# A third batch's keys loaded and pooled in the prologue of a fused pooled-attention and two-layer kernel

## The chip, the cores and the metric

The kernel runs on one core of one Trainium2 chip. The metric is the device time of one execution in microseconds (us), shown as the median of several executions. The engines are TensorE (PE, matmuls), VectorE (DVE), ScalarE (ACT), GpSimd (POOL) and SyncE (SP). In this kernel SyncE issues every DMA, in the order in which the program lists them.

## The reference

Batch 8, 8 heads, 576 tokens, head size 64. Keys and values are averaged over groups of 8 tokens, which leaves 72 of each per head.

```
k_p = k.reshape(B, H, 72, 8, D).mean(axis=3);  v_p likewise
scores = q @ k_p.T / sqrt(D);  attn = softmax(scores)
x = (attn @ v_p), laid out as 4608 tokens x 512
h = relu(x @ w_in1);  x = (h * h) @ w_out1
h = x @ w_in2;  g = h if h >= 1, 0 if h <= -1, else (h + 1)**2 / 4
out = g @ w_out2
```

Both inner layers are 512 -> 2048 -> 512.

## The kernel before

**Chunks.** The 4608 tokens are cut into nine chunks of 512. For a chunk the kernel computes attention by tiles of up to 128 tokens, then the first layer's 16 hidden blocks (f = 0 to 15): a hidden product `h_mm` of 12 matmuls (`hp`, lines 633 to 635), an activation (`act1`), and two blocks later a `y_step` of 12 matmuls (`y`, lines 671 to 675). Finished y banks are copied by `y_out` (`yo`, two buffers) and stored to `x2T`. The second layer follows over all chunks. Numbers are split into a high and a low part, so that each product takes three matmuls.

**Batches and chunks.** A batch has 576 tokens, so chunk 0 is batch 0; chunk 1 is the last 64 tokens of batch 0 and the first 448 of batch 1; chunk 2 has the last 128 tokens of batch 1 as its first tile and then 384 tokens of batch 2. Each batch needs its keys pooled and transposed and its values pooled and split once.

**Pooling.** `load_k(b, p)` loads the keys of two heads (p = 0 to 3), `load_v(b, g)` a group of values (g = 0 to 2), in a tile `kv` that has one buffer. `k_pool` and `v_pool` add halves three times (`pool8`, lines 365, 367 and 369; GpSimd from the second batch on), into `kp` (four buffers) and `vp`. `k_T` transposes `kp` on PE and ScalarE writes the scaled keys to `kBD`. `v_split` makes `VH` and `VL`, and for g = 2 `LH` and `LL` (two GpSimd multiplications, lines 424 and 426). A load of a new `kv` tile waits until the pooling of the one before has read it.

**Attention of a tile.** `load_q` (two `q` buffers), `t0` (query transposes, `qps`), `t1` (scores, `sps`, then maximum and subtraction), `t3` and `t4` (softmax), `t56` (transposes `aps` and `lps`, and the split into `AH`, `AL`, `LT`), then `pv_pair` (`pvps`).

**The prologue.** Chunk 0's attention, the weights' loading and decoding (`Weights`, 16 blocks, lines 256 to 290), chunk 0's hidden blocks and chunk 1's attention are interleaved by a planner, the class `Order`. Each piece of work is a generator (a chain) that yields the engine it needs and a planned time, or an event that it waits for; the planner takes the earliest, and the order in which it emits is the order of each engine's program. A load's landing is planned by `comes(us)`: the sum of transfers so far, plus `us`, plus 2.0. `keys1` is the chain that loads and pools the second batch's keys and values (b = 1); `keys1_T` transposes those keys. Chunk 1's first groups of x are staged in DRAM (`x1S`, line 623) and brought back by `unstage` (line 598) when the last weights are decoded, since x of chunk 1 lives in buffers that the decoding uses. The last weights (f = 15) land in a buffer that is lent, before that, to chunk 1's first and last tile (`late`).

**Behind the prologue.** `attention_units(c, at)` makes a list of calls with due times, in units of hidden blocks, for chunk c; the main loop over c and f executes those that are due (`do`). For each chunk that meets a new batch it lists the batch's loads, poolings and transposes: the first key load 7 units before the batch's predecessor has its scores. Chunk 2's units run beside chunk 1's blocks, which begin at unit 16. All units due at 16 or before come at the first `do(16)`, behind chunk 1's first hidden product and ahead of the last `y_step` of chunk 0.

Of the kernel before, what the change touches and what calls it, by code (L numbers as in the profile page):

```python
# [48 lines left out]
class Order:  # L49
# [13 lines left out]
    def add(self, gen, rank=0.0):  # L63
        c = [rank, self.now, gen, None, None]
        self.chains.append(c)
        self.go(c)
# [57 lines left out]
def pooled_attention_moe_moe2(  # L124
# [13 lines left out]
    nc = tc.nc  # L138
# [5 lines left out]
    NP = H // 2  # L144
# [44 lines left out]
    for c in range(NC):  # L189
        gs, col = [], 0  # L190
        while col < N:
            t0_ = c * N + col
            b, s = t0_ // S, t0_ % S
# [135 lines left out]
    def kv_tile():  # L329
        return att.tile([P, 2, POOL * D], F32, tag="kv", name="kv")  # L330

    def load_k(b, p, t=None):

        t = kv_tile() if t is None else t
        nc.sync.dma_start(
            out=t[:SP_], in_=k[b, 2 * p:2 * p + 2].rearrange("h (s r) d -> s h (r d)", r=POOL)
        )
        kraw[b, p] = t

    def load_v(b, g, t=None):  # L340

        t = kv_tile() if t is None else t
        for e in range(2):
            r = slice(64 * e, 64 * e + 64)
            if g < 2:
                src = v[b, 4 * g + e:4 * g + e + 3:2, :KA * POOL, :]
                nc.sync.dma_start(out=t[r], in_=src.rearrange("h (s r) d -> s h (r d)", r=POOL))
            else:
                src = v[b, :, KA * POOL:, :]
                nc.sync.dma_start(out=t[r, 0], in_=src.rearrange("h (s r) d -> h s (r d)", r=POOL))  # L350
        vraw[b, g] = t
# [9 lines left out]
    def pool8(eng, t, dst):  # L361
        us = (("POOL", 1.3), ("POOL", 0.8), ("POOL", 0.7)) if eng is nc.gpsimd else (
            ("DVE", 0.7), ("DVE", 0.45), ("DVE", 0.3))
        yield us[0]
        eng.tensor_tensor(out=t[:, :, :256], in0=t[:, :, :256], in1=t[:, :, 256:], op=ALU.add)
        yield us[1]
        eng.tensor_tensor(out=t[:, :, :128], in0=t[:, :, :128], in1=t[:, :, 128:256], op=ALU.add)
        yield us[2]
        eng.tensor_tensor(out=dst, in0=t[:, :, :64], in1=t[:, :, 64:128], op=ALU.add)
# [3 lines left out]
    def k_pool(b, p, eng):  # L373
        kp = att.tile([P, 2, D], F32, tag="kp", name="kp", bufs=4)
        t, dst = kraw.pop((b, p))[:SP_], kp[:SP_]
        yield from pool8(eng, t, dst)
        kp_t[b, p] = kp
# [14 lines left out]
    def v_pool(b, g, eng):  # L392
        t = vraw.pop((b, g))
        w = 2 if g < 2 else 1
        vp = att.tile([P, 2, D], F32, tag="vp", name="vp") if b else lent[7][:, 0, 2 * D * g:2 * D * g + 2 * D]
        if b == 0:
            vp = vp.rearrange("p (a d) -> p a d", d=D)
        vp_t[b, g] = vp
        yield from pool8(eng, t[:, :w], vp[:, :w])

    def v_split(b, g, eng):
        vp = vp_t.pop((b, g))
        if g < 2:
            for e in range(2):
                r = slice(64 * e, 64 * e + 64)
                vh, vl = VH[r, 2 * g:2 * g + 2, e, :], VL[r, 2 * g:2 * g + 2, e, :]
                yield "ACT", 0.33
                nc.scalar.activation(out=vh, in_=vp[r], func=AF.Copy, scale=VSCALE)
                yield "DVE", 0.32
                nc.vector.scalar_tensor_tensor(  # L410
                    out=vl, in0=vp[r], scalar=VSCALE, in1=vh, op0=ALU.mult, op1=ALU.subtract
                )
        else:
            vh = att.tile([P, 1, D], F32R, tag="vlh", name="vlh")
            yield "ACT", 0.27
            nc.scalar.activation(out=vh, in_=vp[:, 0:1], func=AF.Copy, scale=VSCALE)
            vl2 = vp[:, 1:2]
            yield "DVE", 0.23
            nc.vector.scalar_tensor_tensor(
                out=vl2, in0=vp[:, 0:1], scalar=VSCALE, in1=vh, op0=ALU.mult, op1=ALU.subtract  # L420
            )
            mb = mask.rearrange("p (h o) -> p h o", o=1).to_broadcast([P, H, D])
            yield "POOL", 1.1
            eng.tensor_tensor(out=LH, in0=vh.to_broadcast([P, H, D]), in1=mb, op=ALU.mult)
            yield "POOL", 1.1
            eng.tensor_tensor(out=LL, in0=vl2.to_broadcast([P, H, D]), in1=mb, op=ALU.mult)
        order.signal("v", b, g)
# [21 lines left out]
    def at_once(chain):  # L449

        if chain is None:
            return
        value = None
        while True:
            try:
                kind, x = chain.send(value)
            except StopIteration:
                return
            value = None
            if kind == "take":  # L460
                value = order.things[x].pop(0)[1]
# [260 lines left out]
    def attention_units(c, at, stage=(0, 0.5, 1, 1, 2, 2.5, 3)):  # L722

        units = []
        ts = tiles[c]

        def add(s, f, *a):
            units.append((s, lambda: at_once(f(*a))))

        for i, T in enumerate(ts):  # L730
            s = at[i]
            if i:
                add(at[i - 1] + 0.5, load_q, T)
            else:
                add(s - 2, load_q, T)
            add(s + stage[0], t0, T)
            add(s + stage[1], t1, T, 0)
            add(s + stage[1], t1, T, 1)
            add(s + stage[2], t3, T)
            add(s + stage[3], t4, T)  # L740
            add(s + stage[4], t56, T)
            G = T.group
            if T is G.tiles[-1]:
                for p in range(NP):
                    add(s + stage[5 + p // 2], pv_pair, G, p)
            if i + 1 < len(ts) and ts[i + 1].b != T.b:

                b = T.b + 1
                a = s + stage[1]
                add(a - 7, load_k, b, 0)  # L750
                for p in range(NP):
                    add(a - 6 + 1.5 * p, k_pool, b, p, nc.gpsimd)
                    if p + 1 < NP:
                        add(a - 6 + 1.5 * p, load_k, b, p + 1)
                    else:
                        add(a - 6 + 1.5 * p, load_v, b, 0)
                    add(a + 0.5 + p // 2 * 0.5, k_T, b, p)
                e = s + stage[6]
                add(a, v_pool, b, 0, nc.gpsimd)
                add(a, load_v, b, 1)  # L760
                add(e, v_split, b, 0, nc.gpsimd)
                add(e, v_pool, b, 1, nc.gpsimd)
                add(e, load_v, b, 2)
                add(e + 1, v_split, b, 1, nc.gpsimd)
                add(e + 1, v_pool, b, 2, nc.gpsimd)
                add(e + 1.5, v_split, b, 2, nc.gpsimd)
        return units
# [5 lines left out]
    with tc.manual_schedule():  # L773
# [19 lines left out]
        def comes(us):  # L793

            landed[0] = max(landed[0], order.now) + us
            return landed[0] + 2.0
# [23 lines left out]
        def ev(*name):  # L820
            return "ev", name
# [45 lines left out]
        def keys1():  # L867
            for p in range(NP):
                load_k(1, p)
                yield "until", comes(1.3)  # L870
                yield from k_pool(1, p, nc.gpsimd)
                order.signal("kp", p)
            for g in range(3):
                load_v(1, g)
                yield "until", comes(2.2)
                yield from v_pool(1, g, nc.gpsimd)
                yield ev("x", G1[0])
                yield from v_split(1, g, nc.gpsimd)

        def keys1_T():  # L880
            yield ev("scores", T1[0])
            for p in range(NP):
                yield ev("kp", p)
                yield from k_T(1, p)
# [121 lines left out]
        for t in T1:  # L1006
            order.add(tokens(t), RANK[1])
        order.add(keys1(), RANK[1])
        order.add(keys1_T(), RANK[1])
        for g in G1:  # L1010
# [6 lines left out]
        for c in range(2, NC):  # L1017
            n = len(tiles[c])
            stride = 3 if n > 4 else 3.5
            units += attention_units(c, [16 * (c - 1) - 1 + stride * i for i in range(n)])  # L1020
# [91 lines left out]
```

## Time and profile before

| | |
|---|---|
| median of 3 executions | 1809.26 us (1808.73 to 1817.22) |
| profiled execution, device time | 1810.97 us |
| its span, first to last instruction | 1809.2 us |
| PE busy | 1746.8 us (97%) |
| PEld / DVE / ACT / POOL busy | 80% / 41% / 43% / 8% |
| PE, busy tenths in 40 slices of 45 us | 5897699999999999999999999999999999999999 |
| granted PE clock, same slices | 6999799999999999999999999999999999999999 |

A digit of a slice is the busy share in tenths (9 is 90% or more). The clock is in tenths of the full one. In the rows below an idle time in square brackets is that of the engine just in front of the instruction, with what ended it; "x" counts merged instructions.

### The profile page before, as it was taken

To read this page: it belongs to the slowest core of one execution; us is meant where nothing else is said; L and a number is where in the kernel's file an instruction comes from. 1 tells how busy PE (TensorE), PEld (TensorE's weight loads), DVE (VectorE), ACT (ScalarE), POOL (GpSimd) and SP (SyncE) were. 2 spreads that over 40 slices of the span, in tenths; PEclk is the share of its full clock that TensorE was granted. 3 is DMA by queue.
4 is the path that set the end of the run, shared out by engine and by line. 5 is a ranking of instruction groups with operands and counts; after the bars stand their busy time and mean duration, and the time that the engine had idled before them with its cause. 6 is when DMAs were issued, how large, how long until landed. Compare 5 with 4: busy or idle time off the path is not lost.

```text
span 1809.2 us, 20648 instructions
## 1 busy us (share of the span) xinstructions
PE 1746.8 (97%) x8116; PEld 1444.9 (80%) x8116; DVE 739.0 (41%) x1234; ACT 781.5 (43%) x1499; POOL 152.1 (8%) x183
## 2 busy tenths in 40 slices
PE   5897699999999999999999999999999999999999
PEld 4676588888888888878888778888888888888887
DVE  7995243334333343433329933222223323222232
ACT  5784333434434343443348743333333333333333
POOL 3321220211111120210000000000000000000000
PEclk6999799999999999999999999999999999999999
DMA  9532310202111110311026401010101010101000
GB/s 253 175 108 67 89 34 20 67 19 59 31 52 39 38 48 18 82 21 35 1 89 214 163 0 47 1 47 1 47 1 47 1 47 1 47 1 47 0 24 24
DMA packets 89601, 95.18 MB, mean 53 GB/s; under 512 B 43296, under 2 KB 61984, under 8 KB 89504
## 3 DMA queue, kind: packets, MB, share of 16 engines
q1 hardware_dynamic: 89504, 93.87, 17.8%
q8 instruction: 64, 1.05, 0.2%
q14 instruction: 33, 0.27, 0.0%
HBM read 73.66 MB, written 20.19 MB: 52 GB/s over the span
## 4 chain that ended last, share of the span: by engine, by line
PE 86%; DVE 6%; DMA 3%; ACT 2%; issue 2%; SPq 0%; POOL 0%; DVEq 0%; ACTq 0%; POOLq 0%
PE hp L633 13%; PE hp L635 13%; PE hp L634 13%; PE y L684 7%; PE y L683 7%; PE y L682 7%; PE y L671 7%; PE y L672 6%; PE y L675 6%; PE pvps L611 2%; PE sps L502 2%; DVE w L290 1%; DVE wa L275 1%; PE qps L484 1%; PE aps L560 1%
## 5 line engine op out<-in xcount | busy, mean ns | idle before, releaser
L633 PE MATMUL hp<-x,w 128*128 128x512 f32 x1116 | 442.2, 396 | 4.6 <-ACT w L285 2.5
L634 PE MATMUL hp<-x,w 128*128 128x512 f32 x1116 | 435.7, 390 | 0.9 <-DVE w L290 0.8
L635 PE MATMUL hp<-x,w 128*128 128x512 f32 x1116 | 435.7, 390 | 0.0
L633 PEld LDWEIGHTS hp<-x,w 128*128 128x128 f32 x1116 | 210.5, 189 | 49.1 <-DVE u L661 3.0
L661 DVE SCALAR_TENSOR_TENSOR u<-u,hp 128x512 f32<-128x512 f32 x144 | 99.0, 687 | 359.7 <-ACT u L660 359.7
L635 PEld LDWEIGHTS hp<-x,w 128*128 128x128 f32 x1116 | 209.9, 188 | 44.3
L634 PEld LDWEIGHTS hp<-x,w 128*128 128x128 f32 x1116 | 210.7, 189 | 42.9 <-DVE w L290 1.5
L671 PE MATMUL y<-gh,w 128*128 128x512 f32 x576 | 232.3, 403 | 0.0
L672 PE MATMUL y<-gh,w 128*128 128x512 f32 x576 | 226.0, 392 | 0.0
L652 DVE TENSOR_TENSOR gl<-hp,gh 128x512 fp32r<-128x512 f32 x144 | 99.3, 690 | 309.8 <-ACT hp L650 309.7
L684 PE MATMUL y<-w,gl 128*128 128x512 f32 x540 | 210.2, 389 | 0.0
L682 PE MATMUL y<-w,gh 128*128 128x512 f32 x540 | 210.2, 389 | 0.0
L683 PE MATMUL y<-w,gh 128*128 128x512 f32 x540 | 210.1, 389 | 0.0
L659 ACT ACTIVATE u<-hp 128x512 f32<-128x512 f32 x144 | 85.9, 596 | 286.8 <-PE hp L635 286.8
L662 ACT ACTIVATE gh<-u 128x512 fp32r<-128x512 f32 x144 | 91.0, 632 | 173.5 <-PE y L683 148.9
L663 DVE TENSOR_TENSOR gl<-u,gh 128x512 fp32r<-128x512 f32 x144 | 99.8, 693 | 157.7 <-ACT gh L662 152.1
L675 PE MATMUL y<-gl,w 128*128 128x512 f32 x576 | 155.2, 391 | 0.0
L648 ACT ACTIVATE gh<-hp 128x512 fp32r<-128x512 f32 x144 | 86.1, 598 | 120.8 <-PE y L672 119.8
L675 PEld LDWEIGHTS y<-gl,w 128*128 128x128 f32 x576 | 108.7, 189 | 23.3
L641 ACT ACTIVATE hp<-hp 128x512 f32<-128x512 f32 x144 | 85.2, 591 | 97.5 <-PE hp L635 97.2
L671 PEld LDWEIGHTS y<-gh,w 128*128 128x128 f32 x576 | 108.9, 189 | 21.1
L672 PEld LDWEIGHTS y<-gh,w 128*128 128x128 f32 x576 | 108.9, 189 | 20.5
(140 smaller groups left out, 2003.2 us busy)
## 6 DMA issues: line engine op xcount, KB each, us to landing
w<-in_moe_w_in_dram SPq DMA_DIRECT2D x31, 512.0 KB
w<-in_moe_w_out_dram SPq DMA_DIRECT2D x31, 512.0 KB
x2T<-yo SPq DMA_DIRECT2D x36, 256.0 KB
xraw<-x2T SPq DMA_DIRECT2D x9, 1024.0 KB
out_dram<-yo SPq DMA_DIRECT2D x35, 256.0 KB
qraw<-in_q_dram SPq DMA_DIRECT2D x32, 256.0 KB
kv<-in_k_dram SPq DMA_DIRECT2D x28, 288.0 KB
kv<-in_v_dram SPq DMA_DIRECT2D x28, 256.0 KB
```

What stands on the lines that cost most here:

```text
L633: nc.tensor.matmul(out=hp, lhsT=hi[:, cs], rhs=xh[kk], start=(kk == 0), stop=False)
L634: nc.tensor.matmul(out=hp, lhsT=lo[:, cs], rhs=xh[kk], start=False, stop=False)
L635: nc.tensor.matmul(out=hp, lhsT=hi[:, cs], rhs=xl[kk], start=False, stop=(kk == KD - 1))
L652: nc.vector.tensor_tensor(out=gl, in0=hp, in1=gh, op=ALU.subtract)
L661: nc.vector.scalar_tensor_tensor(out=u, in0=u, scalar=1.0, in1=hp, op0=ALU.min, op1=ALU.max)
L663: nc.vector.tensor_tensor(out=gl, in0=u, in1=gh, op=ALU.subtract)
L671: nc.tensor.matmul(out=ys[d], lhsT=hi[:, cs], rhs=gh, start=(f == 0), stop=False)
L672: nc.tensor.matmul(out=ys[d], lhsT=lo[:, cs], rhs=gh, start=False, stop=False)
L675: nc.tensor.matmul(out=ys[d], lhsT=hi[:, cs], rhs=gl, start=False, stop=(f == KF - 1))
L682: nc.tensor.matmul(out=ys[t], lhsT=gh[:, cs], rhs=hi, start=(f == 0), stop=False)
L683: nc.tensor.matmul(out=ys[t], lhsT=gh[:, cs], rhs=lo, start=False, stop=False)
L684: nc.tensor.matmul(out=ys[t], lhsT=gl[:, cs], rhs=hi, start=False, stop=(f == KF - 1))
```

## The change

For the third batch (b = 2) the key loads, the key poolings and the first value load move from chunk 2's units into the prologue, to the end of the chain `keys1`. The other batches' stay where they are (`if b > 2`), and so do the third batch's key transposes, value poolings and splits.

```
                 a = s + stage[1]
-                add(a - 7, load_k, b, 0)
+                if b > 2:
+                    add(a - 7, load_k, b, 0)
                 for p in range(NP):
-                    add(a - 6 + 1.5 * p, k_pool, b, p, nc.gpsimd)
-                    if p + 1 < NP:
-                        add(a - 6 + 1.5 * p, load_k, b, p + 1)
-                    else:
-                        add(a - 6 + 1.5 * p, load_v, b, 0)
+                    if b > 2:
+                        add(a - 6 + 1.5 * p, k_pool, b, p, nc.gpsimd)
+                        if p + 1 < NP:
+                            add(a - 6 + 1.5 * p, load_k, b, p + 1)
+                        else:
+                            add(a - 6 + 1.5 * p, load_v, b, 0)
                     add(a + 0.5 + p // 2 * 0.5, k_T, b, p)
...
                 yield from v_split(1, g, nc.gpsimd)
+            for p in range(NP):
+                load_k(2, p)
+                yield "until", comes(1.3)
+                yield from k_pool(2, p, nc.gpsimd)
+            load_v(2, 0)
 
         def keys1_T():
```

## Rows read from the trace of the kernel before

**Rows 1.** PE's timeline, 175 to 220 us: start, duration, line, operation, count, [idle before].

```profile
189.94 1.11 PE L484 MATMUL qps<-ident,qraw 128*128 128x128 f32 x4 [14.68 <-DMA qraw<-in_q_dram]
...
195.26 0.77 PE L671 MATMUL y<-gh,w 128*128 128x512 f32 x1
...
200.53 0.44 PE L383 MATMUL kps<-ident,kp 72*128 72x72 f32 x2
...
208.20 0.47 PE L611 MATMUL pvps<-AH,VH 128*128 128x128 f32 x1 [3.77 <-DVE AL L572]
...
215.20 0.22 PE L611 MATMUL pvps<-AH,VH 128*128 128x128 f32 x1
...
216.26 0.45 PE L671 MATMUL y<-gh,w 128*128 128x512 f32 x1
...
219.07 0.60 PE L484 MATMUL qps<-ident,qraw 128*128 128x128 f32 x4
```

**Rows 2.** SyncE's timeline: DMA issues, of several merged the first's start and their length.

```profile
26.18 0.40 SPq L335 DMA_DIRECT2D kv<-in_k_dram  x1
...
66.82 1.26 SPq L347 DMA_DIRECT2D kv<-in_v_dram  x2
...
123.77 7.18 SPq L623 DMA_DIRECT2D x1S<-xs  x4
147.20 0.38 SPq L232 DMA_DIRECT2D w<-in_moe_w_in_dram  x1
...
150.51 16.06 SPq L598 DMA_DIRECT2D x<-x1S  x16
166.67 19.21 SPq L335 DMA_DIRECT2D kv<-in_k_dram  x4
185.94 0.40 SPq L355 DMA_DIRECT2D qraw<-in_q_dram  x1
```

**Rows 3.** GpSimd's timeline, 112 to 178 us.

```profile
115.50 1.90 POOL L426 TENSOR_TENSOR LL<-vp,mask 128x512 fp32r<-128x512 f32 x1 [1.02 <-DVE vp L419]
170.91 1.28 POOL L365 TENSOR_TENSOR kv<-kv 72x512 f32<-72x512 f32 x1 [53.52 <-DMA kv<-in_k_dram]
...
176.93 1.26 POOL L365 TENSOR_TENSOR kv<-kv 72x512 f32<-72x512 f32 x1 [3.40 <-DMA kv<-in_k_dram]
```

**Rows 4.** Windows: length, PE, PEld, DVE, ACT, POOL busy, PEclk, DMA; last two POOL's kv.

```profile
120.00:140.00 20.00, 19.15 (x97) 15.50 (x97) 18.60 (x28) 16.98 (x42) 0.00 (x0) 1.00 0.16 54
157.00:160.70 3.70, 1.28 (x6) 0.74 (x4) 3.05 (x3) 2.15 (x3) 0.00 (x0) 1.00 0.01 2
208.20:214.30 6.10, 6.10 (x19) 5.27 (x20) 1.54 (x4) 1.43 (x4) 0.00 (x0) 0.50 0.15 54
240.00:260.00 20.00, 20.00 (x104) 16.95 (x103) 7.64 (x16) 7.64 (x15) 2.48 (x3) 1.00 0.12 29
...
32.50:66.90 34.40, 15.67 (x12) 0.83 0.70 195
170.80:192.00 21.20, 9.74 (x12) 0.73 0.21 54
```

**Rows 5.** Timelines of DVE, PE and ACT: three single instructions with their waits.

```profile
135.39 0.69 DVE L652 TENSOR_TENSOR gl<-hp,gh 128x512 fp32r<-128x512 f32 x1 [1.03 <-ACT hp L650]
160.74 0.50 PE L633 MATMUL hp<-x,w 128*128 128x512 f32 x1 [2.46 <-ACT w L285]
206.21 0.60 ACT L693 ACTIVATE yo<-y 128x512 f32<-128x512 f32 x1 [4.37 <-DMA x2T<-yo]
```

**Rows 6.** VectorE's timeline: two decode steps beside GpSimd's poolings and without them.

```profile
32.66 2.27 DVE L278 CUSTOM_DVE_ANT_0 wa<-w,wa 128x2048 uint16<-128x2048 uint16 x1
43.69 1.21 DVE L278 CUSTOM_DVE_ANT_0 wa<-w,wa 128x2048 uint16<-128x2048 uint16 x1
44.83 0.68 DVE L269 TENSOR_SCALAR wa<-wa 128x1024 f32<-128x1024 f32 x1
63.62 1.72 DVE L269 TENSOR_SCALAR wa<-wa 128x1024 f32<-128x1024 f32 x1
```

## The prediction

> **What bounds the kernel now.** I read the page's busy shares and slices first. TensorE (PE) is busy nearly everywhere, except in the first two slices and in the fourth and fifth, so a gain has to come from one of these holes or from work taken off PE, and this change takes none off. Next, PE's rows in order of time, around the end of the prologue. The second chunk's first hidden product is done at 175.26 us; the next instruction, the query transposes of the third chunk's first tile, starts at 189.94, after 14.68 us of idleness, and what released it is the landing of a query tile, not of a key tile [rows 1]. Third, SyncE's queue tells why the query is late. The four key loads stand in that queue from 166.67 us and take 19.21 us to issue, because there is one buffer for keys and values and each load waits for GpSimd to have pooled the one before. The query's load stands behind the last of them and issues at 185.94 [rows 2]. GpSimd's own rows show the rhythm: a key tile's first addition at 170.91, the next tile's at 176.93, after 3.40 us of waiting for the transfer [rows 3]. Fourth, the windows by stage: PE waits a second time, 3.77 us up to 208.20, and then runs for 6.1 us at a granted clock of 0.50 (1.2 GHz, half of the full 2.4 GHz) [rows 1, 4]. From 240 us on PE is busy 20.00 of 20 us [rows 4], so what is gained before that is kept to the end.
>
> **The change, part by part.** Removed from the second chunk's start: four key loads and four key poolings, and the first value load with it. The query's load then stands right behind the copies that bring staged x back; these end at 150.51 + 16.06 = 166.57 us [rows 2]. The query would land some 4 us later, as it does now (185.94 to 189.94), which is before PE asks at 175.26. So the 14.68 us go. Two smaller things go with them. From the transposes to the first y matmul now takes 5.32 us (189.94 to 195.26), at half clock, but ScalarE's and VectorE's steps in between don't depend on that clock: between 0 and 2.7 us, I take 0.9. The y group from 195.26 to 200.53 takes 5.27 us at half clock; the same group later takes 2.81 us (216.26 to 219.07): 2.46 us [rows 1]. Sum: 14.68 + 0.9 + 2.46 = 18.0 us.
>
> What is late next is the wait of 3.77 us in front of 208.20. It ends when VectorE has written AL, and VectorE stood behind a copy of finished y that waited for an output buffer's store: ScalarE's copy at 206.21 was released by such a store [rows 1, 5]. The query of the next tile and the second value load stand ahead of that store in SyncE's queue; with their cover gone the store goes earlier by a few tenths, but its own transfer stays. So the wait shrinks by 0 to 0.8 us. Whether the clock falls behind it is open: at 157 to 161 us PE waited 2.46 us and the granted clock stayed at 1.00, here it waited 3.77 us and got 0.50 [rows 1, 4, 5]. The ten pvps matmuls and the hidden product behind it take 7.0 us at the low clock (208.20 to 215.20); at full clock 1.06 us (215.20 to 216.26) and, for twelve matmuls, 2.81: 3.1 us less. I take 1.5 us for wait and clock together, nearer to nothing, since a wait of about that length stays. Gain at this place: 19.5 us, bounds 18.0 and 21.9.
>
> Moved to: GpSimd, behind the second batch's last multiplication, which ends at 117.40 us [rows 3]; SyncE, between the last weight loads; and VectorE's busiest stretch. The loads are written where the planner's clock puts them. By its costs a key tile takes 1.3 + 2.0 for the load and 2.8 for the pooling: 6.1 each, 24.4 for four. Behind 117.4 this ends at 141.8, and the last weights' load issues at 147.20 [rows 2, 3], so I expect all five loads to be written ahead of it. Nothing else in the planner's account changes: no PE, ScalarE or VectorE cost, and the sum of transfers has caught up by then. On the chip the second key load can stand behind the first x1S store at 123.77 [rows 2]. The kp buffers of the second batch are long read.
>
> First cost: SyncE's queue ahead of the last weights. They land, are decoded, and PE waits for them at 160.74 [rows 5], so each microsecond that they are late is a microsecond of the end. With a second load at 124.2, a landing of 3.40 us [rows 3] and a pooling of 3.92 us (15.67 over four, in the early prologue, where 9.74 over four is what it takes alone [rows 4]), the third goes at 131.5, the fourth at 138.8, the value load at 146.1 and, after two issues of about 0.4, SyncE is free at 146.9: just in time for 147.20. Cost 0.
>
> Second cost: VectorE. While GpSimd pools, some VectorE instructions last longer, and GpSimd's do too: the decode step on line 278 took 2.27 us beside a pooling and 1.21 us without; the one on line 269 1.72 and 0.68 [rows 6]. So a pooling costs VectorE between 0 (it meets none of these) and about 1.6 us (it meets one of them and part of a second). I take 1.0, four times: 4.0 us. VectorE is busy 18.60 of 20 us from 120 to 140 [rows 4], and one idle stretch of 1.03 us at 135.39 [rows 5] can take some of it. What is left, 3.0 us (bounds 0 and 5.4), delays the second chunk's last tile, to which the code lends the last weights' buffer, so their load, so PE at 160.74. The Trainium skill (GPSIMD Engine Reference, Specifications) says that GpSimd shares its SBUF interfaces with VectorE, in contention with VectorE instructions in a two-port mode or with two SBUF inputs. The two lengthened lines fit that: the one on 278 reads w and wa, both in SBUF [rows 6]. By the rule alone the VectorE instructions that read PSUM would lose nothing, which points below 1.0 for a pooling: at 0.5 the forecast would be 2 us lower.
>
> Third cost: a longer wait at 160.74. 2.46 us kept the full clock; 5.5 us may lose it, and half clock for 6.1 us costs 3.05 us [rows 4, 5]. Between 0 and 3.05, I take 1.5.
>
> Sum: 19.5 - 0 - 3.0 - 1.5 = 15.0 us. The profiled execution had a span of 1809.2 us and took 1810.97; the median of the runs shown is 1809.26, 1.7 us below it. The gain is subtracted from the median: 1794.3 us.
>
> **The rivals.** (A) As above, 0.60; from 1787.4 (21.9 and no cost) to 1799.7 (18.0 - 5.4 - 3.05). (B) Poolings that meet nothing on VectorE and full clock at both places: gain up to 21.9 us, 1787.4 us. For it: from 129 us on part of VectorE's work waits for ScalarE anyway, as at 135.39 [rows 5]. Against: VectorE has almost no gap there, 18.60 of 20 us [rows 4]. 0.15. (C) The queue. In the early prologue four rounds of load and pooling took from 26.18 to 66.82 us, 10.2 each [rows 2]. With such rounds the fifth load goes at 124.2 + 30.6 = 154.8, SyncE is free at 155.6, the last weights are 8.4 us late, and with half of the clock's price the gain is 9.6 us: 1799.7 us. For it: SyncE works in order. Against: from 32.5 to 66.9 us the DMA engines were busy for 0.70 of the time, from 120 to 140 for 0.16 [rows 4]. 0.13. The Trainium skill (DMA: Bandwidth & Descriptors, Anatomy of one DMA) states that a DMA's semaphore wait is held on the issuing sequencer; by it a weight load behind a waiting key load is late by the whole wait, as the query load of before shows. (D) The loads are written behind the copies of staged x after all, or another wait takes the query's place: 1809 us. For it: the order hangs on the planner. Against: 24.4 fits into 29.8. 0.07. (E) Slower: the queue again, decided when the last weights are over 16.4 us late (19.5 less 3.05), which takes rounds of 7.3 + 16.4/3 = 12.8 us; at 16 us a round they would be 26 us late and the time 1817 us. The rounds of the early prologue, at their mean of 10.2, don't reach that. 0.05.
>
> **How the numbers follow.** About 0.5%, 9 us, is what a measurement of this kernel tells from no change. A and B are faster by more, C about half the time: 0.60 + 0.15 + 0.07 = 0.82 faster. The rest of C and D: 0.13 same. E: 0.05 slower. The predicted time is A's. The range from 1787 to 1801 holds A, most of B and most of C, some 0.83.
>
> **What would show it.** Right: no key load on SyncE between 166 and 200 us, the query load right behind the x copies, PE's wait at the third chunk's first transposes below 1 us, GpSimd's key poolings from about 117 to 146 us at 3 to 4 us each, VectorE's lines 269, 278 and 290 longer there, PE's wait for the last weights some 3 us longer. Wrong: the last weights' load more than 6 us later than 147, the query wait still over 5 us, or a new wait of several microseconds in the second chunk.

## The result and the profile after

The changed kernel takes 1794.36 us (median of five executions, 1792.68 to 1801.1) where the kernel before, run beside it, takes 1814.83 (1808.73 to 1817.22). The ratio is 0.9896, with an interval of 0.9878 to 0.9914: faster by 1.0%. The profiled execution took 1792.96 us with a span of 1791.2, so its span is 18.0 us shorter than that of before. The forecast was 1794.3 us, in a range of 1787 to 1801.

The page's slices come first: the busy share of TensorE (PE), and below it the granted clock.

```profile
PE   5898999999999999999999999999999999999999
...
PEclk6999999999999999999999999999999999999999
```

The hole that stood in the fourth and fifth slices of before is nearly filled (the third to sixth digits were 9, 7, 6, 9 and are 9, 8, 9, 9), and the clock's dip in the fifth slice is gone. PE's timeline at that place, and at the last weights of the prologue, in the changed kernel:

```profile
162.90 0.79 PE L633 MATMUL hp<-x,w 128*128 128x512 f32 x1 [2.65 <-ACT w L285]
...
169.02 0.36 PE L611 MATMUL pvps<-AH,VH 128*128 128x192 f32 x1
...
179.69 0.60 PE L484 MATMUL qps<-ident,qraw 128*128 128x128 f32 x4
...
183.78 0.47 PE L671 MATMUL y<-gh,w 128*128 128x512 f32 x1
186.63 0.29 PE L383 MATMUL kps<-ident,kp 72*128 72x72 f32 x2
...
191.69 0.33 PE L611 MATMUL pvps<-AH,VH 128*128 128x128 f32 x1 [1.43 <-DVE AL L572]
...
197.25 0.22 PE L611 MATMUL pvps<-AH,VH 128*128 128x128 f32 x1
```

The query transposes at 179.69 have no bracket: nothing was waited for, against 14.68 us [rows 1]. From there to the first y matmul 4.09 us pass (5.32 before), the y group takes 2.85 us (5.27), the wait for AL is 1.43 us (3.77), and the stretch from the first pvps matmul to the next group of them 5.56 us (7.0). At the last weights PE still waits, 2.65 us where it was 2.46 [rows 5], and the hidden product behind that wait now takes 6.1 us (162.90 to 169.02). In before it took 3.9 us, from 160.74 [rows 5] to the next group's first pvps matmul, on PE's timeline of before:

```profile
164.66 0.25 PE L611 MATMUL pvps<-AH,VH 128*128 128x192 f32 x1
```

SyncE's queue in the changed kernel:

```profile
107.93 0.38 SPq L232 DMA_DIRECT2D w<-in_moe_w_in_dram  x1
...
123.45 0.58 SPq L623 DMA_DIRECT2D x1S<-xs  x1
124.14 0.50 SPq L335 DMA_DIRECT2D kv<-in_k_dram  x1
124.92 0.55 SPq L623 DMA_DIRECT2D x1S<-xs  x1
131.09 0.30 SPq L335 DMA_DIRECT2D kv<-in_k_dram  x1
...
138.83 0.31 SPq L335 DMA_DIRECT2D kv<-in_k_dram  x1
146.72 1.35 SPq L347 DMA_DIRECT2D kv<-in_v_dram  x2
149.16 0.40 SPq L232 DMA_DIRECT2D w<-in_moe_w_in_dram  x1
...
168.77 0.43 SPq L355 DMA_DIRECT2D qraw<-in_q_dram  x1
169.30 1.26 SPq L347 DMA_DIRECT2D kv<-in_v_dram  x2
...
187.39 4.00 SPq L697 DMA_DIRECT2D x2T<-yo  x4
```

No key load is left between 166 and 187 us (the next one goes at 206.59), and the query load stands right behind the copies of staged x, at 168.77 instead of 185.94 [rows 2]. The last weights' load is at 149.16. The two loads of such weights, the last and the one ahead of it, are 41.23 us apart (107.93 to 149.16); before, the same two were 38.28 apart (108.92 to 147.20). This distance, the *slip* where it grows, is the measure used below: executions differ in how early the prologue's last part begins, and the distance leaves that out.

GpSimd's timeline, the third and fourth of its four moved poolings:

```profile
134.72 1.34 POOL L365 TENSOR_TENSOR kv<-kv 72x512 f32<-72x512 f32 x1 [3.66 <-DMA kv<-in_k_dram]
136.14 0.73 POOL L367 TENSOR_TENSOR kv<-kv 72x256 f32<-72x256 f32 x1
136.95 1.85 POOL L369 TENSOR_TENSOR kp<-kv 72x128 f32<-72x128 f32 x1
142.26 1.35 POOL L365 TENSOR_TENSOR kv<-kv 72x512 f32<-72x512 f32 x1 [3.46 <-DMA kv<-in_k_dram]
143.70 1.60 POOL L367 TENSOR_TENSOR kv<-kv 72x256 f32<-72x256 f32 x1
145.37 1.32 POOL L369 TENSOR_TENSOR kp<-kv 72x128 f32<-72x128 f32 x1
```

VectorE's timeline, three instructions beside poolings:

```profile
119.33 1.10 DVE L272 TENSOR_SCALAR wa<-wa 128x1024 int32<-128x1024 int32 x1
...
143.35 1.36 DVE L290 TENSOR_TENSOR w<-wa,w 128x1024 fp32r<-128x1024 f32 x1
144.63 1.75 DVE L275 SCALAR_TENSOR_TENSOR wa<-w,wa 128x1024 int32<-128x1024 int32 x1
```

The smallest addition of a pooling, on line 369, lasted 1.85 and 1.32 us where 0.46 is its usual time; the decode step on line 275 beside it took 1.75 us, 1.23 elsewhere, line 272's 1.10 against 0.69. Both sides pay. The windows (columns as in [rows 4]) behind the two waits of after:

```profile
162.90:169.00 6.10, 5.63 (x12) 4.08 (x13) 1.21 (x1) 0.00 (x0) 0.00 (x0) 0.50 0.50 129
191.70:197.25 5.55, 5.55 (x22) 4.61 (x23) 1.35 (x4) 1.36 (x4) 0.00 (x0) 0.69 0.14 50
```

The granted clock is 0.50 and 0.69. Behind AL it was 0.50 before [rows 4]; behind the last weights it was 1.00, as this window of before shows:

```profile
160.70:166.80 6.10, 5.31 (x27) 4.32 (x28) 1.94 (x3) 1.20 (x3) 0.00 (x0) 1.00 0.49 129
```

The low clock (1.2 GHz) now stands behind the last weights, and behind AL it is held for part of the stretch only.

### The profile page after: what moved, and what is told of

Read it like the earlier page. It is cut to its first block, busy times and chain, and to the rows that moved or that the text cites. A ratio compares the mean times of both kernels' runs of the same rounds, so it can differ in the third digit from the quotient of the medians.

```text
span 1791.2 us, 20650 instructions
## 1 busy us (share of the span) xinstructions
PE 1743.7 (97%) x8116; PEld 1442.2 (81%) x8116; DVE 739.7 (41%) x1234; ACT 781.4 (44%) x1499; POOL 158.2 (9%) x183
## 4 chain that ended last, share of the span: by engine, by line
PE 87%; DVE 8%; DMA 2%; issue 2%; ACT 1%; SPq 0%; DVEq 0%; ACTq 0%
PE hp L633 14%; PE hp L634 13%; PE hp L635 13%; PE y L684 7%; PE y L682 7%; PE y L683 7%; PE y L671 7%; PE y L672 6%; PE y L675 6%; PE pvps L611 2%; PE sps L502 2%; DVE w L290 1%; DVE wa L275 1%; DVE wa L278 1%; DVE wa L269 1%
```

## The experiments

Each ratio is to the kernel before, timed in the same job. Four runs stood beside a before of 1815.54 us: the query load alone, only the last addition, GpSimd's additions alone, and the value and query loads behind the first stores. The other four stood beside one of 1811.79.

**The query load alone.** From before: only the place of the query's load is changed, ahead of the key loads.

```
-                add(s - 2, load_q, T)
+                add(s - 7 if c == 2 else s - 2, load_q, T)
```

> The kernel before, with one query load moved: chunk 2's first query is listed ahead of the third batch's key loads in SyncE's queue, nothing else. Theory (the whole serial chain of the one kv buffer stands in the second chunk, and the query was only its first victim): the query transposes start at about 175.3 us without a wait, but the last key transposes wait for the fourth pooling at about 192 us, and the stores of finished y still stand behind the second value load at about 201 us, so AL is written at about 208 us as before and the gain is 0 to 3 us: 1806 to 1809 us. Rival (the query's place in the queue is the whole cause): the 14.68 us go, some 1794 us.

1815.52 us, ratio 1.0007 (0.9994 to 1.002): nothing gained. PE's timeline of it:

```profile
184.19 0.60 PE L484 MATMUL qps<-ident,qraw 128*128 128x128 f32 x4
...
199.19 0.38 PE L383 MATMUL kps<-ident,kp 72*128 72x72 f32 x1 [5.62 <-POOL kp L369]
...
214.97 0.47 PE L611 MATMUL pvps<-AH,VH 128*128 128x128 f32 x1 [9.51 <-DVE AL L572]
```

The query's wait is gone, and its time comes back elsewhere: 0.59 and 5.62 us of waiting for the last two pooled keys, 9.51 us for AL instead of 3.77, and 2.2 us at the last weights, where the clock of this execution was 0.51 (in before 1.00). So the query's place in the queue is not the cause; the chain of four loads and poolings is, and it has to leave this place, at least in part, for PE to gain.

**Only the last addition of each pooling.** From the changed kernel; the first additions of the third batch's key pooling are left out, so its keys are sums over fewer elements.

```
-                yield from k_pool(2, p, nc.gpsimd)
+                kp = att.tile([P, 2, D], F32, tag="kp", name="kp", bufs=4)
+                t = kraw.pop((2, p))[:SP_]
+                yield "POOL", 0.7
+                nc.gpsimd.tensor_tensor(out=kp[:SP_], in0=t[:, :, :64], in1=t[:, :, 64:128], op=ALU.add)
+                kp_t[2, p] = kp
```

> The changed kernel with the third batch's four key poolings cut to the last of their three additions (the third batch's keys are then not the means). Theory (poolings lengthen VectorE's decode steps by some 3 us in the prologue, which delays the last weights): the last weights' load issues 2 to 3 us earlier than in the changed kernel (149.2 us there), PE's product behind them starts 2 to 3 us earlier, and the time falls by 2 to 5 us, the clock behind that wait included: 1788 to 1792 us. Rival (the decode is not what delays them): no change, 1793 to 1795 us.

1793.72 us, ratio 0.9888 (0.9868 to 0.9907), and the weight loads are 41.83 us apart (108.90 to 150.73), no less than in the changed kernel. The theory's saving did not come. The trace says what took its place: the shorter rounds let the value load go at 134.81 instead of 146.72, and the value pooling that it releases met the decode of the last weights, on VectorE's timeline:

```profile
140.35 1.79 DVE L269 TENSOR_SCALAR wa<-wa 128x1024 f32<-128x1024 f32 x1
142.17 1.11 DVE L272 TENSOR_SCALAR wa<-wa 128x1024 int32<-128x1024 int32 x1
```

Alone these take 0.69 us each. The edit brought other GpSimd work into that decode, so it decided nothing by itself.

**The same without the value load there.** As above, and the first value load goes back to where before had it.

```
+                if b == 2:
+                    add(a - 1.5, load_v, b, 0)
...
-            load_v(2, 0)
```

> The changed kernel with the third batch's key poolings cut to their last addition (its keys are then not the means) and the first value load listed where it was before the change. So neither key nor value poolings load GpSimd between 117 and 147 us; the key loads stay. Theory (the slip of the last weights is made by GpSimd's additions beside VectorE's decode, plus some by a key load in front of an x1S store): the last weights' load stands 38 to 39.5 us behind the load before it (38.3 before the change, 41.2 in the changed kernel), and the time falls by 2 to 5 us: 1788 to 1792 us. Rival (the loads alone make the slip): 41 us between the two loads, 1793 to 1795 us.

1790.29 us, ratio 0.9879 (0.9865 to 0.9894). The two weight loads are 38.47 us apart (110.93 to 149.40), the distance of before: the slip is gone. The median is 2.8 us below that of the changed kernel in the same job (1793.07), which is a hint only, since the two ratios' intervals overlap (0.9865 to 0.9894 and 0.9883 to 0.9913). The rival is refuted only in part: with the shorter poolings the loads moved too. The second key load now goes ahead of all x1S stores and the third at 128.01 us, behind the second of them, so that no key load stands just ahead of that store as it does in the changed kernel (124.14, then 124.92). What the additions cost and what the load costs is told apart further down.

**GpSimd's additions alone.** From before, with no load moved: eighteen additions in place on a value buffer whose contents have been used, behind the second batch's value work, 18.3 us of POOL time (118.5 to 138.2), where the moved poolings take 14.8.

```
+            t = vraw[1, g][:, :1]
...
+            for _ in range(6):
+                yield from pool8(nc.gpsimd, t, t[:, :, :64])
```

> The kernel before, with 18 more additions on GpSimd at the end of the prologue's key and value chain (six poolings of a tile of 128 x 256 that is already there, some 9 us of GpSimd's time when alone; results unused). No load, no queue and no other engine is touched. Theory (GpSimd's work costs VectorE): VectorE slips by 2 to 4 us behind 117 us, the last weights' load goes from 147.2 to 149 to 151 us, and the time rises by 2 to 6 us: 1811 to 1815 us against 1809. Rival (the cost in the changed kernel comes from SyncE's queue): no change, 1809 us.

1813.79 us, ratio 0.9995 (0.9984 to 1.0007). VectorE's timeline of it:

```profile
122.09 1.65 DVE L275 SCALAR_TENSOR_TENSOR wa<-w,wa 128x1024 int32<-128x1024 int32 x1
123.77 1.37 DVE L278 CUSTOM_DVE_ANT_0 wa<-w,wa 128x2048 uint16<-128x2048 uint16 x1
...
134.11 0.95 DVE L269 TENSOR_SCALAR wa<-wa 128x1024 f32<-128x1024 f32 x1
```

The lengthening is there (0.42, 0.14 and 0.26 us in these rows, about 2.4 us over all of VectorE's instructions up to the last weights' load), and the weight loads stand 39.47 us apart (110.08 to 149.55): a slip of 1.19 us, which the times don't tell from nothing. The theory had 2 to 6 us. A part of the lengthening was taken up by VectorE's idle stretch of 1.03 us [rows 5], which this trace no longer has. The Trainium skill (GPSIMD Engine Reference, Specifications) puts the contention at VectorE instructions in a two-port mode or with two SBUF inputs; lines 275 and 278, with w and wa in SBUF, fit it [rows 6]. Lines 269 and 272 read one tile, and no run here shows whether they ran in such a mode. The cost to the path is the 1.19 us of this run.

**Loads behind all stores of x1S.** From the changed kernel: key loads two to four wait for the first tile's x to be finished.

```
             for p in range(NP):
+                if p == 1:
+                    yield ev("x", G1[1])
                 load_k(2, p)
```

> The changed kernel with the second, third and fourth key load listed behind all four x1S stores. The x1S stores then have no key load beside them; but the chain of loads and poolings starts some 6.5 us later, and the value load and with it the last weights, which stand behind it in SyncE's queue, can go only when the fourth pooling is done, at about 151 us. Theory (a load that waits in front of the last weights costs what it waits): the last weights issue at about 152 us, 3 us later than in the changed kernel, and PE's product behind them with them: 1796 to 1798 us. Rival (the last weights wait for their buffer anyway, the order of the loads doesn't matter): 1793 to 1795 us.

1799.9 us, ratio 0.9937 (0.9921 to 0.9954): 6.8 us above the unchanged version beside it. SyncE's queue:

```profile
132.15 15.91 SPq L335 DMA_DIRECT2D kv<-in_k_dram  x3
154.82 1.36 SPq L347 DMA_DIRECT2D kv<-in_v_dram  x2
156.28 0.56 SPq L232 DMA_DIRECT2D w<-in_moe_w_in_dram  x1
```

PE's timeline at the last weights:

```profile
171.22 0.79 PE L633 MATMUL hp<-x,w 128*128 128x512 f32 x1 [9.95 <-ACT w L285]
```

The weights now stand behind a value load that waits for the last key tile, and PE waits 9.95 us for them, where it waits 2.84 in the unchanged version of the same job. So the prediction's rival of the queue was a real mechanism: loads a few places later in the queue decide. The theory expected some 3 us, since it put the end of the fourth pooling at about 151 us; by its own delay of 6.5 us the value load of the changed kernel (146.72) would go at 153.2, and it went at 154.82. The Trainium skill (DMA: Bandwidth & Descriptors, Anatomy of one DMA) states that a DMA's semaphore wait sits on the issuing sequencer; this run agrees, the weights' load going 0.1 us after the value load's issue is over (154.82 + 1.36).

**Value and query loads behind the first stores.** From the changed kernel, to test why AL comes sooner: the second value load and the second tile's query load are listed behind the first two stores of finished y.

```
-                add(at[i - 1] + 0.5, load_q, T)
+                add(at[i - 1] + (1.25 if c == 2 and i == 1 else 0.5), load_q, T)
...
-                add(a, load_v, b, 1)
+                add(a + 0.75 if b == 2 else a, load_v, b, 1)
```

> The changed kernel, with the second value load and the second tile's query load of chunk 2 listed behind the first two stores of finished y in place of ahead of them, so that their transfers run beside the stores. Theory (a store's landing takes about 2 us alone and about 4.4 us beside these loads, which is why PE's wait for AL fell from 3.77 to 1.43 us): PE's wait for AL grows to 3 to 4 us and the time by 1.5 to 4 us: 1795 to 1798 us. Rival (the wait fell since the copies themselves came earlier): the wait stays near 1.4 us, no change.

1796.17 us, ratio 0.9899 (0.9882 to 0.9916), and the wait for AL is 1.44 us as in the changed kernel. The time lies in the theory's range, but the ratio is that of the changed kernel (0.9896). Loads right behind a store cost it nothing; the theory fails as it was put here. Loads in front of it were not tested by this edit.

**Two key tiles here, two there.** From the changed kernel: only two key tiles in the prologue, the other two and the first value load right behind the copies of staged x, with the query load ahead of them.

```
-            for p in range(NP):
+            for p in range(2):
+                if p == 1:
+                    yield ev("x", G1[1])
...
+        load_q(tiles[2][0])
+        for p in (2, 3):
+            load_k(2, p)
+            at_once(k_pool(2, p, nc.gpsimd))
+        load_v(2, 0)
```

> A version meant to be faster than the changed kernel. Only the first two key tiles are loaded and pooled in the prologue, the second behind the x1S stores; the other two, with chunk 2's first query ahead of them, right behind the copies of staged x, where VectorE is idle; the second value load is listed behind the stores of finished y. Theory (the changed kernel pays about 3 us on VectorE and in the store queue, and about 2 us of low clock behind a longer wait): the last weights' load stands about 39 us behind the load before it, the last key transposes still don't wait, and the time falls by 2 to 5 us: 1788.5 to 1792 us. Rival (key tiles three and four come too late, or the value load does): a wait of several microseconds at the last key transposes or at AL, 1795 us or more.

1793.21 us, ratio 0.9899 (0.9882 to 0.9915): no better. The slip shrinks as expected (115.29 to 154.77, 39.48 us), PE waits for neither the query nor the keys, but AL's wait is 1.72 us and the clock behind it 0.70, as the window shows:

```profile
196.50:202.10 5.60, 5.56 (x22) 4.68 (x23) 1.47 (x4) 1.41 (x4) 0.46 (x1) 0.70 0.55 155
```

The unchanged version beside it had 1.44 us and 1.00 there (below). From the load ahead of the last weights' to the end 1680.5 us pass here (115.29 to 1795.8) and 1680.8 there (109.39 to 1790.2), so most of what the shorter slip saved, 1.46 us, is given back later, by these two as far as the profiles tell.

**The changed kernel once more,** unchanged, in the job of three runs above: the same without the value load, loads behind all stores of x1S, and two key tiles here, two there.

> The changed kernel itself, as the base for the three beside it on the same chip, and a second profiled execution. Theory: 1793 to 1796 us, the last weights 41 us behind the load before them, and a granted clock of about 0.5 behind the wait for them, as in the first profile. Rival (the low clock there was that one execution's): full clock, and some 2 us less.

1793.07 us, ratio 0.9898 (0.9883 to 0.9913). The weight loads stand 40.94 us apart, the query is not waited for, AL's wait is 1.44 us. The clock is what differs from the first profile, in the same two windows, and neither the theory's 0.5 nor the rival's full clock is what stands behind the last weights:

```profile
164.20:170.30 6.10, 5.31 (x19) 4.14 (x19) 1.23 (x1) 0.46 (x1) 0.00 (x0) 0.72 0.48 127
192.10:197.60 5.50, 5.50 (x34) 4.95 (x35) 1.63 (x5) 1.90 (x7) 0.00 (x0) 1.00 0.14 51
```

## Why the prediction was right, step by step

**The query's wait.** Right: 14.68 us of the gain, none of it left. The run with only the query moved adds why: it is the chain of loads, not the query's own place.

**Transposes to y, and the y group.** The first went from 5.32 to 4.09, a gain of 1.23 us against the 0.9 taken; the second from 5.27 to 2.85, 2.42 against 2.46.

**What is late next: the term that was mis-sized.** "So the wait shrinks by 0 to 0.8 us" and "I take 1.5 us for wait and clock together". The wait shrank by 3.77 - 1.43 = 2.34 us, the stretch behind it by 7.0 - 5.56 = 1.44: 3.8 us. With that the gain at this place is 14.68 + 1.23 + 2.42 + 3.8 = 22.1 us, above the upper bound of 21.9. (That bound keeps the 0.9 fixed; with that term's own bounds of 0 and 2.7 the place would have had 17.1 to 23.7.) The step that failed is "the store goes earlier by a few tenths, but its own transfer stays". In before, SyncE's queue stood so:

```profile
191.95 9.09 SPq L347 DMA_DIRECT2D kv<-in_v_dram  x4
201.09 0.60 SPq L355 DMA_DIRECT2D qraw<-in_q_dram  x1
201.73 6.16 SPq L697 DMA_DIRECT2D x2T<-yo  x4
```

ScalarE's two copies of finished y, before (the second is in [rows 5]):

```profile
199.49 0.60 ACT L693 ACTIVATE yo<-y 128x512 f32<-128x512 f32 x1 [1.19 <-PE y L675]
```

And in the changed kernel:

```profile
186.78 0.59 ACT L693 ACTIVATE yo<-y 128x512 f32<-128x512 f32 x1
...
189.51 0.60 ACT L693 ACTIVATE yo<-y 128x512 f32<-128x512 f32 x1 [1.33 <-DMA x2T<-yo]
```

Before, the copy ended at 199.49 + 0.60 = 200.09 and its store was issued at 201.73: 1.64 us late, behind a value load that waited for its buffer and a query load. After, the copy ends at 187.37 and the store goes at 187.39. The transfer did not stay either: from the store's issue to the copy that it releases 4.48 us before (201.73 to 206.21), 2.12 after (187.39 to 189.51). In the traces with the two loads as before just in front of the store it is 4.48 (before), 4.53 (the query alone) and 4.60 (GpSimd alone); in six with neither shortly in front of it (they had been issued over 8 us earlier, or came behind) 2.10 to 2.13; with the two issued 3.8 and 2.4 us ahead of it (two and two) 2.60. What the DMA engines did in these two stretches, before and in the changed kernel (columns as in [rows 4], the last two the share and the GB/s of DMA):

```profile
201.73:206.21 4.48, 2.70 (x15) 2.03 (x13) 0.00 (x0) 0.11 (x2) 1.35 (x2) 1.00 1.04 272
187.39:189.51 2.12, 2.12 (x11) 1.70 (x10) 0.78 (x2) 0.74 (x4) 0.00 (x0) 1.00 0.55 206
```

Before, the engines were busy throughout and moved some 1220 KB (4.48 us at 272 GB/s) where a store has 256; after, some 440 KB. So the store shared them with the loads ahead of it. The stores of x1S, of the same size, show the same: with a key load just ahead, the second of them released ScalarE's fourth copy of x 5.15 to 5.68 us after its issue (three profiles), without one 4.06 to 4.32 (the four others in which that copy waited for it). No run put the value and the query load back with nothing else changed, so for this part, 2.4 us, the traces show the cause but no edit isolates it. Of the 1.6 and 2.4 us the wait shows 2.34: before, the first copy began 1.04 us ahead of the end of the y group (199.49 and 200.53), now 0.15 us behind it (186.78 and 186.63).

**First cost, the queue.** Right at 0, and by the written times: the third key load at 131.09 (131.5 said), the fourth at 138.83 (138.8), the value load at 146.72 (146.1). The last weights' load then waited 1.1 us, until PE's last `lps` transpose had read its buffer, and not for the queue. The run with the loads behind the stores shows the edge: its weight loads stood 46.94 us apart against 40.94 in the unchanged version, 6.0 us more, PE's wait was 7.1 us longer, and the time 6.8.

**Second cost, VectorE.** The size was right, 2.95 us for 3.0, but a good third of it came from elsewhere. Lined up at the end of the second batch's last multiplication (117.40 before, 116.52 after), VectorE's last softmax product ahead of the weights slipped from 27.44 to 30.46, 3.0. Six VectorE instructions in between last longer than before, by 1.8 us in all: lines 272 and 275 beside the first pooling by 0.41 and 0.14, lines 290 and 275 beside the fourth by 0.15 and 0.54, and two small ones by some 0.27 each. That is 0.44 us for a pooling, where the prediction took 1.0. The other 1.2 us are ScalarE's fourth copy of x for staging, for which VectorE waits 1.34 us. ScalarE's row in the changed kernel says what the copy waited for:

```profile
130.35 0.39 ACT L619 ACTIVATE xs<-pvps 128x256 fp32r<-128x256 f32 x1 [3.26 <-DMA x1S<-xs]
```

Before, that copy waited 2.03 us for VectorE's gl. Now it waits for the second x1S store, issued at 124.92 behind a key load at 124.14. Two runs test this part. In both, the loads behind all stores of x1S and two and two, no key load stands between the stores, and the copy waits as in before; ScalarE's row of the first of them:

```profile
130.54 0.38 ACT L619 ACTIVATE xs<-pvps 128x256 fp32r<-128x256 f32 x1 [2.03 <-DVE gl L652]
```

From the end of the last multiplication the copy came 12.60 and 12.62 us later in these two, 13.83, 13.54 and 14.07 in the three with a key load ahead of the second store: the load beside the store costs 0.9 to 1.5 us. And with two poolings and no such load (two and two) the slip is 1.20 us, no more than VectorE's lengthening in that trace (1.2 us). So the prediction was right by two errors that met: 1.2 us too much for VectorE and nothing for the store, whose neighbour it had named ("the second key load can stand behind the first x1S store") without a price.

**Third cost, the clock.** From the wait's end to the next group's first pvps matmul 3.9 us before (160.74 to 164.66), 6.1 after: 2.2 us for the 1.5 taken, within its bounds of 0 and 3.05. But the reason given did not come. The wait was to grow to 5.5 us, and it grew from 2.46 to 2.65: 2.9 of the 3.1 us that PE lost up to here stand ahead of it, as other waits (half of them for A, at the `aps` transposes: 1.87 us instead of 0.37). The clock fell all the same. After a wait of 2.46 it was 1.00 in two profiles, after one of 2.50 it was 0.50, after one of 2.49 it was 0.72, so the length of this wait does not tell it, and that the term came near is luck. In the second profile of the changed kernel it cost 1.5 us (164.24 to 169.65 is 5.4), since the clock there was 0.72 and not 0.50.

**The sum.** 14.68 + 1.23 + 2.42 + 3.8 - 2.95 - 2.2 = 17.0 us. The spans differ by 18.0; the 1.0 that is left is the earlier start of the prologue's last part (108.92 and 107.93), which differs between executions. The prediction's 15.0 lacked the 2.3 us at AL. That the median nevertheless met its 1794.3 is luck: the gain was subtracted from 1809.26, while five executions of before gave 1814.83 and the gain between medians is 20.5 us. What of that goes beyond 17 us is not accounted for by the two profiles.

**The rivals.** No cost at all (1787.4) did not come: VectorE, the store and the clock did charge. The queue's rival did not occur as written, but its mechanism did when the loads were put behind the stores. The query's wait was not replaced by another. The slower case would have taken rounds of 12.8 us; they were 7.0 to 7.9 (124.14, 131.09, 138.83, 146.72).

## What to carry to other kernels

A wait that ends on one late transfer can be the end of a whole chain of loads through one buffer: moving the late transfer alone moved the wait to the chain's next reader here, and only moving the chain, all or half of it, paid. Where a chain is moved into a queue, write down each issue time behind it: the first weights or stores that stand behind a load decide, and here 6 us in the queue cost 6.8. And of a wait that "stays", split its length into issue and landing: both halves may hang on the loads that the change takes away.

## What the runs showed of the hardware

- The same wait is followed by different clocks. Behind the last weights the waits were 2.46 to 2.84 us long in nine profiles; the granted clock of the next 6 us was 1.00 in two of them, 0.72 in two and 0.50 or 0.51 in five. In the tenth profile (loads behind all stores of x1S) the wait was 9.95 us and the clock 0.62. Behind AL, waits of 1.42 to 1.72 us were followed by 0.69 to 1.00, those of 3.65 to 9.51 by 0.50.
- GpSimd suffers more than VectorE where the two meet: a 0.46 us addition took 1.85 us, a 1.23 us decode step 1.75. Over the four moved poolings GpSimd took 14.8 us for 9.7 [rows 4], VectorE lost 1.8. On the path, 18 us of GpSimd work cost 1.19 us.
- A store of finished y took 2.1 us or 4.5 us from its issue to the copy that it releases, in two groups, with only one run's 2.60 in between.
- Executions of one kernel differ by some 10 us (before: 1809.1 to 1819.16 in the 23 of one job), and part of that arises before the prologue's last part, whose first weight load began between 107.93 and 115.29 us in the ten traces. In the three late ones (113.77, 115.10 and 115.29) ScalarE's third small copy of x for staging, at 85 to 87 us, had waited 8.9 to 10.2 us for a store of x1S; in the other seven it waited 1.1 to 3.9.
